# Both MLP products of a retention and MLP kernel as pairs of 64-column halves of the TensorE array

## The chip, the cores and the metric

The kernel runs on one core of a Trainium2 chip. The metric is device time in microseconds (us), median over several executions. Executions of one kernel in one job spread over 1 to 2%; a run that lies over 1.5% above the fastest of its kernel is called slow and is left out of the ratios. A comparison is given as a ratio: the mean time of one kernel's fast runs over that of the other's fast runs of the same rounds, so not quite the ratio of the medians that stand beside it.

## The reference, cut to what matters

```python
def _attn_ref(q, k, v):                       # 8 batches, 8 heads, 576 positions, 64 per head
    scores = scale * np.matmul(q, k.transpose(0, 1, 3, 2))
    ret = scores * Dmat                       # gamma_h ** (i - j) where i >= j, else 0
    return np.matmul(ret, v)

def _moe_ref(x, w_in, w_out):                 # 4608 tokens, 512 -> 2048 -> 512
    h = x @ w_in
    g = h * np.clip(h + 3.0, 0.0, 6.0) / 6.0
    return g @ w_out
```

The retention's output, heads side by side, is the MLP's input.

## The kernel before

The retention is done in chunks of 128 positions with a running state; the MLP follows in blocks of 512 tokens. Chunks and MLP are interleaved by hand: one long list of tokens fixes the order of instructions on every engine. *Tiling* means that TensorE's array (128\*128 in the profile, active rows by active columns) is used as two halves at once: row tiling (64\*128) splits the rows, column tiling (128\*64) the columns. In the kernel before, the two halves of an output pair (column tiling) or of a score pair (row tiling) mostly start 3 to 4 ns apart, and an output pair of 128 columns starts every 55.7 ns. A *semaphore* is, in the built programs, a counter that one instruction raises and another waits for. Per chunk:

- three loads on SP's DMA queue (q, k, v), and casts to 16 bit on GpSimd and VectorE;
- one transposing DMA for q and k, issued from ScalarE's queue, in ScalarE's stream (28 in all, ACTq in the profile);
- scores (row tiling, 64*128 in the profile), then outputs and state (column tiling, 128*64) on TensorE.

The MLP's two products use the whole array (128*128). ScalarE and VectorE turn each sum of the first product into g. In 8 of the 9 blocks the second product is made as seven products of sub-blocks with 256 columns (accA to accD in the profile), in the other as a plain one (po).

```python
def xpose(c):                                     # ScalarE's queue
    qk = qk16s[c]
    qt = work.tile([P, 8, P], FP16, tag="qkT", bufs=4, name="qkT")
    nc.scalar.dma_start_transpose(qt, qk.rearrange("p a h d -> p (a h d)"))
...
# outputs of the retention: two halves of 64 columns, z = 0 and 1
nc.tensor.matmul(xp[rows[z], p, :], vt[:, 2 * p + z, :], at[:, z, p, :], ...)
...
def up(kb, fc):                                   # first product of the MLP
    ph = psum.tile([P, BLK], FP32, tag="mm", bufs=4, name="ph")
    for m in range(NCC):
        nc.tensor.matmul(ph, win16[:, m, P * fc:P * fc + P], xt[:, m, :],
                         start=(m == 0), stop=(m == NCC - 1))
    hswish(ph, g[:, fc, :])                       # ScalarE, then VectorE
```

## Time and profile before

| | before |
|---|---|
| time, median of the first 3 runs | 307.52 us (304.84 to 307.79) |
| span of the profiled run | 302.4 us |
| TensorE busy | 290.4 us, 96% |
| transfers | 54 MB; the 16 DMA engines are busy nearly throughout to about 205 us |

The thing to read is that TensorE is the bound by its own busy time, and that transfers are full beside it over the first two thirds. Three of the ten lines on TensorE's waits, from the profile of before: who waited for whom, us in total, times, longest.

```profile
PE sc L283 <- ACT qkT L268: 1.1, 1, 1.1
PE xp L308 <- ACT xt L338: 1.0, 2, 0.8
PE ph L377 <- DVE g L365: 1.0, 2, 0.5
```

None of the ten is over 1.4 us in total, and all but 0.2 us lie before 77 us.

### The profile page before, as it was taken

What the parts mean: (1) busy time and instruction counts of PE and PEld (TensorE: products, weight loads), DVE (VectorE), ACT (ScalarE), POOL (GpSimd) and SP (SyncE); (2) the same over time, 40 slices, a digit from 0 to 9 for tenths busy, and PEclk for the clock granted to TensorE, in tenths of its full rate; (3) what the DMA queues carried; (4) which work ended last, traced back from release to release, by engine and by line L of the source; (5) the groups of instructions that cost most, each with busy time, mean ns of one, the idle gap of its engine ahead of it and who ended that gap; (6) DMA issues with size and microseconds to landing.
All of it is one profiled execution on the core that took longest, in us unless ns stands there. A gap on an engine that the chain in (4) does not pass through costs nothing.

```text
span 302.4 us, 7130 instructions
## 1 busy us (share of the span) xinstructions
PE 290.4 (96%) x2879; PEld 198.8 (66%) x2879; DVE 240.1 (79%) x341; ACT 145.8 (48%) x267; POOL 103.3 (34%) x116
## 2 busy tenths in 40 slices
PE   8789898998999999999999999999999999999995
PEld 3565354787788888547854786468656864684584
DVE  6765843989978999798788997998699768857963
ACT  2786705764237733565157424753467226405610
POOL 5254535776158625463843142334200000000000
PEclk9999999999999999999999999999999999999999
DMA  6999899999999999999999999997503130013003
GB/s 232 308 350 386 195 300 211 221 212 215 281 174 197 224 232 227 190 193 240 242 192 264 238 217 182 255 200 96 160 14 58 37 106 0 1 46 95 2 0 139
DMA packets 149729, 53.93 MB, mean 178 GB/s; under 512 B 134849, under 2 KB 145089, under 8 KB 149697
## 3 DMA queue, kind: packets, MB, share of 16 engines
q1 hardware_dynamic: 120128, 46.15, 69.4%
q10 hardware_dynamic: 29568, 7.34, 18.3%
q8 instruction: 22, 0.36, 0.5%
q14 instruction: 11, 0.08, 0.1%
HBM read 36.70 MB, written 9.44 MB: 153 GB/s over the span
## 4 chain that ended last, share of the span: by engine, by line
PE 85%; SPq 6%; DMA 4%; DVE 3%; ACT 1%; issue 0%
PE ph L377 29%; PE accB L491 10%; PE accA L491 9%; PE accC L491 9%; PE ph L393 8%; PE accD L491 5%; PE po L420 5%; SPq L547 4%; DMA g<-in_moe_w_out_dram 4%; PE xp L308 4%; PE sc L283 3%; PE xp L314 2%; DVE g L365 1%; DVE ss L455 1%; PE state L333 1%; SPq L248 1%
## 5 line engine op out<-in xcount | busy, mean ns | idle before, releaser
L360 ACT ACTIVATE u<-ph 128x512 f32<-128x512 f32 x144 | 84.7, 597 | 63.9 <-PE ph L377 43.8
L365 DVE SCALAR_TENSOR_TENSOR g<-u,ph 128x512 f16<-128x512 f32 x144 | 94.9, 684 | 23.8 <-ACT u L360 23.0
L377 PE MATMUL ph<-xt,win 128*128 128x512 f16 x368 | 82.5, 379 | 1.0 <-DVE g L365 1.0
L377 PEld LDWEIGHTS <-win 128*128 128x128 f16 x432 | 41.5, 98 | 49.0 <-issue 1.6
L491 PEld LDWEIGHTS <-ss 128*128 128x128 f16 x512 | 49.0, 98 | 7.1 <-DVE ss L455 1.1
L176 POOL TENSOR_TENSOR qk<-st,tq 128x512 f16<-128x512 f32 x29 | 31.7, 1095 | 49.7 <-PE state L333 17.8
L176 POOL TENSOR_TENSOR v<-st,tkv 128x512 f16<-128x512 f32 x29 | 31.7, 1097 | 36.0 <-DMA st<-in_v_dram 18.3
L294 DVE TENSOR_TENSOR at<-sc,mask 128x1024 f16<-128x1024 f32 (+1 forms) x34 | 39.0, 1154 | 4.6 <-PE sc L283 4.5
L491 PEld LDWEIGHTS <-g 128*128 128x128 f16 x384 | 36.9, 98 | 6.1 <-issue 0.8
L393 PE MATMUL ph<-xt,win 128*128 128x256 f16 x288 | 33.1, 273 | 0.0
L176 POOL TENSOR_TENSOR qk<-st,tkv 128x512 f16<-128x512 f32 x26 | 28.7, 1105 | 8.5 <-DMA st<-in_k_dram 8.2
L491 PE MATMUL accA<-wout,g 128*128 128x256 f16 x256 | 30.6, 273 | 0.8 <-DVE g L365 0.8
L491 PE MATMUL accB<-tmat,ss 128*128 128x256 f16 x256 | 30.7, 273 | 0.2 <-DVE ss L455 0.2
L393 PEld LDWEIGHTS <-win 128*128 128x128 f16 x288 | 27.6, 98 | 3.6
L338 ACT ACTIVATE xt<-xp 128x512 f16<-128x512 f32 x32 | 19.1, 597 | 19.2 <-PE xp L314 16.6
L455 DVE TENSOR_TENSOR ss<-g 128x1024 f16<-128x1024 f16 (+1 forms) x30 | 23.6, 799 | 0.3
L308 PE MATMUL xp<-at,v 128*64 128x128 f16 x288 | 20.2, 225 | 1.2 <-ACT xt L338 1.0
L308 PEld LDWEIGHTS <-v 128*64 128x64 f16 x288 | 14.4, 109 | 6.9 <-issue 3.5
L511 ACT COPY osb<-accA 128x512 f32<-128x512 f32 x8 | 4.7, 586 | 28.4 <-PE accA L491 28.4
L344 ACT CAST s<-state 64x256 f16<-64x256 f32 x48 | 17.3, 361 | 0.5
L420 PE MATMUL po<-wout,g 128*128 128x512 f16 x64 | 15.0, 379 | 0.6 <-DVE g L365 0.5
L491 PE MATMUL accC<-tmat,ss 128*128 128x256 f16 x128 | 15.4, 273 | 0.0
(88 smaller groups left out, 270.4 us busy)
## 6 DMA issues: line engine op xcount, KB each, us to landing
st<-in_v_dram SPq DMA_DIRECT2D x32, 256.0 KB, 6.4
out_dram<-osb SPq DMA_DIRECT2D x32, 256.0 KB, 4.5
st<-in_q_dram SPq DMA_DIRECT2D x28, 256.0 KB, 5.6
st<-in_k_dram SPq DMA_DIRECT2D x28, 256.0 KB, 5.7
wst<-in_moe_w_in_dram SPq DMA_DIRECT2D x4, 512.0 KB, 7.3
tmat<-in_moe_w_in_dram SPq DMA_DIRECT2D x4, 512.0 KB, 8.0
wst<-in_moe_w_out_dram SPq DMA_DIRECT2D x4, 512.0 KB, 12.5
g<-in_moe_w_out_dram SPq DMA_DIRECT2D x4, 512.0 KB, 6.5
```

Of the source, the lines that this page charges most:

```text
L176: eng.tensor_tensor(out=dst, in0=st[:, ix, :, :], in1=tab.unsqueeze(2).to_broadcast([P, H, D]), op=ALU.mult)
L294: nc.vector.tensor_tensor(out=dst, in0=src, op=ALU.mult, in1=m[:, :].unsqueeze(1).to_broadcast([P, n, P]))
L308: nc.tensor.matmul(xp[rows[z], p, :], vt[:, 2 * p + z, :], at[:, z, p, :], start=(p == 0), stop=False, skip_group_check=True)
L338: nc.scalar.activation(xts[b][:, :, t * P:(t + 1) * P], xp, ACTF.Copy, scale=0.125)
L344: nc.scalar.copy(s16[rows[z], :, rows[z]], sp[rows[z], :, :])
L360: nc.scalar.activation(u, ph, ACTF.Relu, bias=0.5, scale=1.0 / 6.0)
L365: nc.vector.scalar_tensor_tensor(out=dst, in0=uv, scalar=1.0, in1=pv, op0=ALU.min, op1=ALU.mult)
L377: nc.tensor.matmul(ph, win16[:, m, P * fc:P * fc + P], xt[:, m, :], start=(m == 0), stop=(m == NCC - 1))
L393: nc.tensor.matmul(ph[:, 256 * j:256 * j + 256], win16[:, m, P * fc:P * fc + P], xt[:, m, cs], start=(m == 0 and j == 0), stop=(m == NCC - 1),
L420: nc.tensor.matmul(po, g[:, fc, P * mc:P * mc + P], wout16[:, fc, :], start=(fc == 0), stop=(fc == NFC - 1))
L455: nc.vector.tensor_tensor(out=dst, in0=a, in1=c, op=op)
L491: nc.tensor.matmul(ps[:, m, :], lhs(fc, m), rhs[:, fc, :], start=(first and fc == 0 and m == 0), stop=(fc == HF - 1 and m == 1), skip_grou ...
```

## The change

Its intent: where MLP matmuls meet the retention's outputs and states, TensorE changes its tiling, at 94 ns from the full array to columns and 103 ns back in the kernel before. With the MLP in the same 128*64 tiling those changes fall away. Four call sites change alike; one is shown.

```diff
+    def mul(ps, lhs, rhs, start, stop):
+        for z in range(2):
+            nc.tensor.matmul(ps[z * D:z * D + D], lhs[:, z * D:z * D + D], rhs,
+                             start=start, stop=stop, skip_group_check=True)
+
     def up(kb, fc, nwarm=0):
 ...
         for m in range(NCC):
-            nc.tensor.matmul(ph, win16[:, m, P * fc:P * fc + P], xt[:, m, :],
-                             start=(m == 0), stop=(m == NCC - 1))
+            mul(ph, win16[:, m, P * fc:P * fc + P], xt[:, m, :],
+                m == 0, m == NCC - 1)
 ... (the same in up_half, the plain down product and the seven products)
```

More of the change, by code (lines that the diff above doesn't have):

```diff
@@ L392, in up_half @@
             for m in range(NCC):
-                nc.tensor.matmul(ph[:, 256 * j:256 * j + 256],
-                                 win16[:, m, P * fc:P * fc + P], xt[:, m, cs],
-                                 start=(m == 0 and j == 0), stop=(m == NCC - 1),
-                                 skip_group_check=True)
+                mul(ph[:, 256 * j:256 * j + 256],
+                    win16[:, m, P * fc:P * fc + P], xt[:, m, cs],
+                    m == 0 and j == 0, m == NCC - 1)
         d = fcs[1] - fcs[0]
@@ L419, in down_plain_part @@
             for mc, po in enumerate(pos):
-                nc.tensor.matmul(po, g[:, fc, P * mc:P * mc + P],
-                                 wout16[:, fc, :],
-                                 start=(fc == 0), stop=(fc == NFC - 1))
+                mul(po, g[:, fc, P * mc:P * mc + P], wout16[:, fc, :],
+                    fc == 0, fc == NFC - 1)
     def down_plain_end(kb, pos):
@@ L490, in product @@
             for m in range(2):
-                nc.tensor.matmul(ps[:, m, :], lhs(fc, m), rhs[:, fc, :],
-                                 start=(first and fc == 0 and m == 0),
-                                 stop=(fc == HF - 1 and m == 1),
-                                 skip_group_check=True)
+                mul(ps[:, m, :], lhs(fc, m), rhs[:, fc, :],
+                    first and fc == 0 and m == 0, fc == HF - 1 and m == 1)
         if name == "P1":
```

## The prediction

> **What bounds the kernel now.** I read the page's engine shares first, then its slices, then the chain of work that ended last, then busy time by stretch, and last the timeline of TensorE around its changes of tiling.
>
> ```profile
> PE 290.4 (96%) x2879; PEld 198.8 (66%) x2879; DVE 240.1 (79%) x341; ACT 145.8 (48%) x267; POOL 103.3 (34%) x116
> PE   8789898998999999999999999999999999999995
> DVE  6765843989978999798788997998699768857963
> PEclk9999999999999999999999999999999999999999
> PE 85%; SPq 6%; DMA 4%; DVE 3%; ACT 1%; issue 0%
> ```
>
> TensorE is busy for 96% of the span at its full granted clock, and 85% of the chain that ended last is its matmuls. The other 15% is queue, transfer and some VectorE work, all of the first 31 us but for a few pieces up to 77 us (at 68.8 us the chain goes through ScalarE and VectorE for 8.6 us while the first sums for the second product are built). Stretches, each with busy time of TensorE, weight loads, VectorE, ScalarE and GpSimd, then clock and transfers:
>
> ```profile
> 31.00:77.00 46.00, 42.92 (x405) 28.71 (x403) 35.39 (x49) 24.29 (x41) 27.61 (x26) 1.00 1.13 224
> 77.00:122.00 45.00, 44.79 (x594) 37.80 (x593) 40.39 (x50) 20.08 (x40) 23.37 (x22) 1.00 1.31 222
> 122.00:183.00 61.00, 61.00 (x619) 40.22 (x618) 52.67 (x71) 30.07 (x57) 27.17 (x25) 1.00 1.24 221
> 183.00:245.00 62.00, 62.00 (x647) 41.19 (x645) 53.17 (x75) 30.34 (x58) 11.54 (x12) 1.00 0.63 119
> 245.00:302.00 57.00, 53.61 (x365) 35.26 (x362) 38.93 (x55) 21.60 (x37) 0.00 (x0) 1.00 0.17 50
> ```
>
> From 77 to 298 us TensorE is hardly ever idle as the profile counts it (61.00 us busy of 61.00, 62.00 of 62.00). But ends of matmuls are modelled: a 128x256 matmul is listed with 273 ns while the next one starts 109 ns later, so lost time hides under "busy". Only start times show it:
>
> ```profile
> 98.82 0.49 PE L393 MATMUL ph<-xt,win 128*128 128x256 f16 x3
> 99.24 0.41 PE L308 MATMUL xp<-at,v 128*64 128x128 f16 x8
> 99.49 0.29 PE L333 MATMUL state<-v,qk 128*64 128x64 f16 x8
> 99.71 0.40 PE L283 MATMUL sc<-qkT 64*128 64x128 f16 x8
> 100.04 5.41 PE L393 MATMUL ph<-xt,win 128*128 128x256 f16 x48
> 105.38 0.25 PE L308 MATMUL xp<-at,v 128*64 128x128 f16 x2
> 105.46 0.22 PE L314 MATMUL xp<-qkT,s 128*64 128x128 f16 x2
> ```
>
> Columns: start, length, line, and before the shape the tiling. The 48 matmuls of the MLP (128*128) last 5.41 us with one modelled tail of 0.273, so one starts every (5.41 - 0.273)/47 = 0.109 us. The last starts at 105.18; the output matmul (128*64) follows at 105.38, 0.20 later instead of 0.109: 0.09 us are lost at the change of tiling. I did the same for every pair of successive starts in the trace, taking off N/2.4 + 2.4 ns for a stream of N columns. Inside a tiling the median rest is 0 ns (a pair of 64-column halves counted as one). At a change it is, by kind: full array to columns 94 ns (14 times), columns to full 103 (26), full to rows 96 (25), rows to full 96 (13), rows to columns 93 (22), columns to rows 103 (10). That is 110 changes; at these medians 10.7 us, some 3.5% of the span, with the few long waits for data that fall on a change left out.
>
> [...] 93 to 104 ns per change, and output pairs 128 columns long start every 55.7 ns, what one full matmul of that length would take (128/2.4 + 2.4). [...] The trace has 110 ns for a load of 64 columns against 98 for a full one of 128; yet the state pairs (64 columns long) start every 32 ns with two such loads per pair, so loads overlap and don't bind at 109 ns. [...] the trace has 109.1 ns for 256 and 215.8 for 512. [...]
>
> **The change part by part.**
>
> 1. *Doubled instructions, same streaming.* 1680 full MLP matmuls (432 of the up product and 64 of the plain down product with 512 columns; 288 up halves and 896 of the seven-product down part with 256) become 3360. Each pair streams the same columns through both halves of the array at once. If the second starts within 2 to 4 ns of the first, as the output pairs do, a pair takes the 109.1 or 215.8 ns of the full matmul: change 0.
>
> 2. *Changes of tiling removed.* The order of the program stays; VectorE, ScalarE, GpSimd and the queues keep their instructions. Where MLP and outputs or states meet, both are now 128*64: all 26 columns-to-full and 13 of the 14 full-to-columns changes go (the 14th follows a transpose). 3 of these lie before 31 us, where loads set the pace. On the path: 24 x 103 + 12 x 94 = 2.47 + 1.13 = 3.60 us.
>
> 3. *Changes that stay under another name.* The scores remain 64*128. 22 full-to-rows become columns-to-rows (96 to 103 ns: +0.15 us), 12 rows-to-full become rows-to-columns (96 to 93: -0.04).
>
> 4. *Changes added.* Transposes on TensorE and warm-up matmuls stay 128*128, and now sit alone between MLP matmuls: 5 columns-to-full and 3 net full-to-columns, 8 in all, counted in the instruction order of the new kernel. Two, around the warm-up at 22.6 us, are in the load-bound part. 6 x 98 = +0.59 us.
>
> 5. *First pair after a change.* The second output pair after a change starts 80 ns after the first, not 56 (+24), and after a change to the full array the second matmul comes 10 ns late. Entries to columns go from 36 to 38 and those to the full array from 39 to 6, so at most 33 x 10 ns = 0.3 us are won; I count 0.1.
>
> Sum: -3.60 + 0.15 - 0.04 + 0.59 - 0.1 = -3.0 us. Changes fall from 110 to 79, 31 x 98 ns = 3.04, the same by another count. All of it falls between 31 and 245 us; after that only MLP remains and nothing changes.
>
> Does it reach the end? TensorE waits for next to nothing from 77 us on, and must not run into its suppliers when it is ahead by up to 3 us. The transposed q and k of each chunk land 2.5 to 11.5 us before their scores start (smallest 2.52 at 123.9 us, 2.90 at 208.6, 2.82 at 231.1); at 124 us it is ahead by only about 1.2 us, at 231 by almost 3 (but loads and buffers freed by TensorE move forward too). VectorE is at most 90% busy in any stretch (40.39 of 45 us). I take nearly all as kept: about 302.4 - 3.0 = 299.4 us of profiled span.
>
> **The rivals.**
> *The feed of instructions.* A 256-column pair asks for four instructions in 109 ns, 54.5 ns per matmul. [...] The densest stretch before is 256 instructions from 111.86 us in 6.67 us, 26 ns each with no stall; [...] I give it 5%.
> *Pairs a little dearer.* 1680 pairs times 2 ns of extra start-up is 3.4 us and would eat the whole gain: about 307.5. Against it: the output pairs show 55.7 ns, no extra.
> *Pairs a little cheaper.* If each half ran on without the fixed 2.4 ns, 1680 x 2.4 = 4.0 us more would be won: about 300. The same 55.7 ns speaks against it.
> *Gain lost in waits.* If VectorE, 90% busy from 77 to 122 us, takes up part of it, 1 to 2 us remain: about 306.
>
> **Range and chances.** The three times before are 307.52, 304.84 and 307.79, and the profiled run took 304.54: two levels 3 us apart, as large as the effect. From the median, 307.52 - 3.0 = 304.5; since the new runs may fall on either level, I say 304.3, with 301 to 309 as the range. Faster by over 2% needs 6.2 us, twice the sum: 0.04. Slower by over 2% needs the feed to bind or pairs to cost 5 ns more: 0.09. Within 2%: 0.87.
>
> **What would show it right or wrong.** Right: 79 changes of tiling of 93 to 104 ns each, none between MLP and outputs or states; 256-column pairs of the MLP still start every 109 ns and 512-column ones every 216; the last stretch, from the first matmul of the up product after the last output to the end, keeps its length; the span is shorter by about 3 us, gathered evenly from 31 to 245 us. Wrong: [...] second halves that start well after the first (no overlap); pauses between MLP matmuls at steady distances (fetching of a doubled program); weight loads that stretch far beyond 110 ns; or new TensorE waits for VectorE or the transposed q and k.

The N/2.4 + 2.4 ns in it is an estimate, the line through starts in the trace of the kernel before: 109.1 ns for 256 columns and 215.8 for 512. At 128 columns it gives 55.7 ns, and 62 of the 74 spacings between full-array matmuls of that length (TensorE's transposes) are 55 or 56 ns there.

## The result, and the profile after

| | before | after |
|---|---|---|
| median, 4 runs each | 306.18 us | 315.69 us (314.07 to 316.40) |
| ratio after / before | | 1.030 (95%: 1.022 to 1.039) |
| span of the profiled run | 302.4 us | 313.5 us |

The change makes the kernel 3% slower. The page of the changed kernel: busy time, TensorE by slices, its granted clock, and the chain that ended last.

```profile
PE 292.2 (93%) x4559; PEld 222.5 (71%) x4559; DVE 238.1 (76%) x341; ACT 143.3 (46%) x267; POOL 103.7 (33%) x116
PE   8799998998999979829899999999999999999994
PEclk9979999999999999968999999999999999999999
PE 73%; DMA 6%; DVE 5%; SPq 5%; ACT 4%; POOL 3%; issue 2%; ACTq 1%; POOLq 0%
```

TensorE has a hole of which there was none before: slices 15 to 20 of 40, 110 to 157 us, with a "2" at its worst. The granted clock drops just after it, to 0.6 as the mean of slice 18. The chain has lost 12 points of TensorE, and the time from 94 to 139 us now runs through SP's queue, loads, casts and a transpose. So the first look says it is not the matmuls. Who makes TensorE wait now:

```profile
PE ph L361 <- DVE g L371: 6.7, 2, 6.3
PE sc L283 <- DMA qkT<-qk: 2.1, 1, 2.1
PE accB L361 <- DVE ss L459: 2.0, 3, 0.9
```

One wait of 6.3 us and several of 1 to 2 us. The matmuls themselves do what was predicted. Timeline of TensorE, columns as in the prediction:

```profile
103.74 1.26 PE L361 MATMUL ph<-xt,win 128*64 128x256 f16 x20
104.83 0.22 PE L308 MATMUL xp<-at,v 128*64 128x128 f16 x2
...
105.28 0.29 PE L333 MATMUL state<-v,qk 128*64 128x64 f16 x8
105.40 1.92 PE L361 MATMUL accA<-wout,g 128*64 128x256 f16 x32
107.25 0.40 PE L283 MATMUL sc<-qkT 64*128 64x128 f16 x8
```

The MLP follows the four state pairs (32 ns each from 105.28, so 0.13 us) at 105.40: no change of tiling is paid there. I sorted all start times from 60 us on, as in the prediction, with a pair counted as one, and split the time between starts:

| from 60 us to the last matmul, us | streaming | changes of tiling | waits | half clock | rest | sum |
|---|---|---|---|---|---|---|
| before | 226.5 | 8.6 (89) | 1.3 | 0.0 | 2.0 | 238.4 |
| after | 226.8 | 5.4 (56) | 13.1 | 1.8 | 2.1 | 249.1 |

Streaming is the same, the changes of tiling give 3.2 us back as forecast, and waits take 11.8 us and the clock 1.8. The clock drop comes after the idleness: the trace's clock records have half the clock (0.50) from 136.3 to 143.1 us, beginning 3.8 us after the last matmul before the 6.3 us, and the ten 512-column pairs that follow mostly start 427 ns apart instead of 216. The kernel before has no such wait and no such drop between 60 us and its end. That the one causes the other is read from this order, not tested.

**Where the longest wait comes from.** TensorE waits for VectorE, and VectorE for ScalarE:

```profile
138.39 1.88 DVE L371 SCALAR_TENSOR_TENSOR g<-u,ph 128x512 f16<-128x512 f32 x3 [6.93 <-ACT u L366]
```

ScalarE around that time, before and then after; ACTq is its queue, which issues the transpose in order with the activations:

```profile
125.90 1.29 ACT L360 ACTIVATE u<-ph 128x512 f32<-128x512 f32 x2
126.67 1.25 ACTq L184 DMA_TRANSPOSE qkT<-qk  x1
128.03 1.75 ACT L360 ACTIVATE u<-ph 128x512 f32<-128x512 f32 x3 [0.83 <-DVE g L365]
```

```profile
129.46 1.08 ACT L366 ACTIVATE u<-ph 128x512 f32<-128x512 f32 x2
135.81 1.85 ACTq L184 DMA_TRANSPOSE qkT<-qk  x1
137.76 2.06 ACT L366 ACTIVATE u<-ph 128x512 f32<-128x512 f32 x4 [7.22 <-issue]
```

Before, the 13th transpose goes out 0.1 us after the last activation has started. After, it stands in ScalarE's stream from 130 to 135.8 us, and the activations behind it stand with it: 7.22 us of idleness, which the profile can only call "issue". Its casts were ready: the last one of that chunk began at 119.25 and took 2.02 us. So it waited for something that is neither a cast nor an engine.

The built programs tell what. Each has 208 DMAs, 180 on SP's queue and 28 on ScalarE's, and each DMA raises one of eight semaphores at its landing, 26 DMAs to a semaphore. In the common order of both queues the eight come in turn, all 208 times in both programs. From the ninth on, a DMA first waits until the DMA that had its semaphore before has landed: this wait is written out for all 200 in the changed kernel and for 199 of 200 in the kernel before. The streams of ScalarE, VectorE, GpSimd and SP are the same in both programs, instruction by instruction. But the common order is not: the transposes stand elsewhere among SP's 180 DMAs. The number, counted from 0, of SP's DMA that stands just ahead of each of the 28 transposes:

```
transpose   1  2  3  4  5  6  7  8  9 10 11 12  13  14  15  16  17 ...  21  22 ... 28
before     42 44 50 51 58 60 66 72 76 77 81 86  91  96 103 107 114     136 141    155
after      44 46 53 56 62 64 71 80 83 85 89 93 101 106 112 117 124     146 150    155
later by    2  2  3  5  4  4  5  8  7  8  8  7  10  10   9  10  10      10   9      0
```

In these programs a later place means that the semaphore was held by a later DMA. The 13th transpose now waits for the landing of this SP issue (the first of the two):

```profile
129.82 1.84 SPq L161 DMA_DIRECT2D st<-in_k_dram  x2
```

By the trace's record it landed at 135.74 us; the transpose went out at 135.81. In the kernel before, the holder ahead of it had landed 3.07 us before ScalarE came to it. Of the 28 transposes, 9 go out within 0.12 us of such a landing in the changed kernel (of five loads, three stores and one transpose), and none in the kernel before (the two nearest come 0.16 and 0.22 us after it).

**Why the build reorders.** Only the TensorE instructions differ, so something that the build derives from them sets the order; its own estimate of TensorE's time is the likeliest. Built without running: pairs in the first product alone move the 13th transpose by 5, in the second alone by 4, in both by 10. An estimate that counts the two halves one after the other would fit this, but this is argued.

### The profile page after: what moved, and what is told of

Its sections match the earlier page's. It is cut to its first block, busy times and chain, and to the rows that moved or that the text cites.

```text
span 313.5 us, 10492 instructions
## 1 busy us (share of the span) xinstructions
PE 292.2 (93%) x4559; PEld 222.5 (71%) x4559; DVE 238.1 (76%) x341; ACT 143.3 (46%) x267; POOL 103.7 (33%) x116
## 4 chain that ended last, share of the span: by engine, by line
PE 73%; DMA 6%; DVE 5%; SPq 5%; ACT 4%; POOL 3%; issue 2%; ACTq 1%; POOLq 0%
PE ph L361 32%; PE accB L361 8%; PE accC L361 7%; PE accA L361 7%; PE po L361 4%; PE accD L361 4%; SPq L156 4%; DVE g L371 3%; PE xp L308 2%; DMA st<-in_v_dram 2%; PE sc L283 2%; DMA st<-in_k_dram 2%; PE xp L253 2%; DVE ss L459 2%; DMA st<-in_q_dram 2%; POOL qk L176 2%
## 5 line engine op out<-in xcount | busy, mean ns | idle before, releaser
L361 PE MATMUL ph<-xt,win 128*64 128x512 f16 (+1 forms) x1312 | 118.2, 337 | 6.8 <-DVE g L371 6.7
L361 PEld LDWEIGHTS <-win 128*64 128x64 f16 x1440 | 82.0, 111 | 48.4 <-issue 9.5
L361 PEld LDWEIGHTS <-ss 128*64 128x64 f16 x1024 | 54.8, 110 | 4.5 <-DVE ss L459 4.3
L361 PEld LDWEIGHTS <-g 128*64 128x64 f16 x896 | 48.6, 110 | 7.6 <-issue 1.2
L176 POOL TENSOR_TENSOR qk<-st,tkv 128x512 f16<-128x512 f32 x26 | 29.4, 1129 | 10.1 <-DMA st<-in_k_dram 5.9
L361 PE MATMUL accB<-tmat,ss 128*64 128x256 f16 x512 | 30.8, 273 | 2.0 <-DVE ss L459 2.0
L361 PE MATMUL accA<-wout,g 128*64 128x256 f16 x512 | 30.7, 273 | 0.0
L361 PE MATMUL accC<-tmat,ss 128*64 128x256 f16 x256 | 15.7, 273 | 0.6 <-DVE ss L459 0.6
L283 PE MATMUL sc<-qkT 64*128 64x128 f16 x256 | 12.7, 219 | 3.2 <-DMA qkT<-qk 2.1
L361 PE MATMUL po<-wout,g 128*64 128x512 f16 x128 | 15.1, 380 | 0.6 <-DVE g L371 0.5
L361 PE MATMUL accD<-tmat,g 128*64 128x256 f16 x256 | 15.4, 273 | 0.0
```

The lines of the kernel that those rows point to most:

```text
L176: eng.tensor_tensor(out=dst, in0=st[:, ix, :, :], in1=tab.unsqueeze(2).to_broadcast([P, H, D]), op=ALU.mult)
L283: nc.tensor.matmul(sc[z][:, p, :], qt[z * D:z * D + D, HP + p, :], qt[z * D:z * D + D, p, :], start=True, stop=True)
L361: nc.tensor.matmul(ps[z * D:z * D + D], lhs[:, z * D:z * D + D], rhs, start=start, stop=stop, skip_group_check=True)
```

## The experiments

Theory 1: the loss is in the places of the transposes in the common order of DMAs, through the shared semaphores. Theory 2: the loss is in the pairs, either their number or their feed or the lead that they give TensorE over its suppliers.

To separate them, the places are pinned by ordering edges that exist in the build alone and add no wait on the chip. The other 4 engines keep the hand-made order, SP's DMAs are chained in their traced order. With the old places the full-array kernel builds to the same streams and waits as the kernel before, which shows that the pinning by itself changes nothing.

```diff
+    PLACE = [42, 44, 50, ...]
+    for y, x in zip(sp_list, sp_list[1:]):
+        tc.add_manual_dep(x.ins, y.ins.name, nosync, reason="as traced")
+    for x, n in zip(xp_dma, PLACE):
+        tc.add_manual_dep(x.ins, sp_list[n].ins.name, nosync, reason="place")
+        if n + 1 < len(sp_list):
+            tc.add_manual_dep(sp_list[n + 1].ins, x.ins.name, nosync, reason="place")
```

All runs below have right results unless said otherwise.

### Each kernel with the other's places

The changed kernel with the places of before:

> The changed kernel, all MLP matmuls as pairs, but the 28 transposing DMAs of ScalarE stand in the build's common order of DMAs where the kernel before had them, so the eight completion semaphores are dealt out as before. Theory 1 (the loss is in the places: each DMA waits for the landing of the one that had its semaphore before, and in the changed kernel the transposes stand up to 10 DMAs later and so wait for later loads, with ScalarE stuck behind them): about 303 us, 3 less than the kernel before, and no TensorE wait over 2 us after 60 us. Theory 2 (the loss is in the pairs themselves: instructions twice as many, their fetching, or TensorE running ahead of its suppliers): still 313 to 317 us.

The kernel before with the places of the changed kernel:

> The kernel before, full-array MLP matmuls, but the transposing DMAs stand where the changed kernel has them. Theory 1: slow like the changed kernel or a little slower, 313 to 319 us, with a wait of TensorE of several us near 130 to 140 us that goes back to a transpose on ScalarE's queue. Theory 2: as before, 305 to 308 us.

| MLP | places | median us | ratio to before |
|---|---|---|---|
| pairs | old | 304.0 | 0.995 (0.990 to 0.999) |
| full array | new | 314.19 | 1.030 (1.025 to 1.034) |

The times go with the places and not with the matmuls. The full array at the new places is as slow as the changed kernel, with a 5.2 us wait of TensorE at 137 us. Theory 2 falls as the cause of the 3%. It keeps a share: by the same split by start times, one profile each, the full array at the new places has 8.6 us of waits and 1.3 us at half clock, the pairs at the same places 13.1 and 1.8, which the 3.2 us of fewer changes of tiling only partly pay for. Some waits come with the pairs. One execution of the pairs, the profiled one, took 1031.54 us, with the matmuls several times slower (the 512 of accA from wout and g were busy for 110.0 us, 30.7 in the changed kernel) and no clock line on its page; it is a disturbed execution that I can't explain, and it is set aside. The other five were 303.07 to 304.85.

### Half of the shift, and other doses

> The changed kernel with each transposing DMA half way between its old and its new place (0 to 5 DMAs later than before instead of 0 to 10). Theory 1: between the two, 303 to 310 us, with shorter waits at fewer places. Theory 2: still 313 to 317 us.

310.08 us, ratio 1.015 (1.009 to 1.021): half the shift, half the loss.

Three earlier than before, and two later:

> The pairs with every transposing DMA up to the 21st standing 3 DMAs earlier than in the kernel before. If only late places hurt, 302 to 304 us, as good as the old places or better. If the old places are a balance (an early place makes a later load wait for the transpose instead), slower than the old places: 304 to 308 us, with longer waits of SP for transposes.

> The pairs with the transposing DMAs standing 2 DMAs later than in the kernel before. Half way (0 to 5 later) gave 310 and the old places 304, so by the dose 304 to 308 us; 302 to 304 if the old places are on the early side of the best.

Three earlier: 310.37 us, 1.013 (1.006 to 1.020), above the 304 to 308 that I had expected for a balance. SP's queue then waited 28.7 us in sum for transposes, against 6.6 us at the old places (profile of the repeated run below), 13.4 in the kernel before and none in the changed kernel: the old places are a balance, and an early transpose holds up the load that gets its semaphore next. Two later: 308.13 us, ratio 1.000 (0.990 to 1.010); unclear, as its runs spread from 305 to 310, and the slowest of the four counts as slow and isn't in the ratio. How many transposes are held does not measure the loss: here nine went out within 0.12 us of the landing that they waited for, as many as in the changed kernel. How long ScalarE stands does better: its longest idle time just before a held transpose is 2.2 us here, 5.3 in the changed kernel and 8.5 in the next run.

### One transpose alone

> The kernel before (full array) with one transposing DMA, the 13th, placed 10 DMAs later, as the changed kernel has it (the 14th moves 5 to stay behind it). Theory 1: the 13th is issued near 135 us instead of 126.7, when the load that had its semaphore before has landed; ScalarE stands still from about 127 to 135, TensorE runs out of free accumulators and waits 4 to 8 us, and the whole is 308 to 313 us. Theory 2: 304 to 307 us, no such wait.

```diff
-    PLACE = [..., 81, 86,  91,  96, 103, ...]
+    PLACE = [..., 81, 86, 101, 101, 103, ...]
```

317.31 us, ratio 1.036 (1.029 to 1.043): one misplaced transpose (and the one behind it) costs as much as all of the changed kernel's (1.030; the intervals overlap). My 308 to 313 was too low. ScalarE, then TensorE's longest wait, in this run:

```profile
126.06 1.29 ACT L369 ACTIVATE u<-ph 128x512 f32<-128x512 f32 x2
135.89 2.91 ACTq L193 DMA_TRANSPOSE qkT<-qk  x1
138.90 2.06 ACT L369 ACTIVATE u<-ph 128x512 f32<-128x512 f32 x4 [11.55 <-DMA out_dram<-osb]
```

```profile
PE ph L386 <- DVE g L374: 10.9, 2, 10.1
```

The transpose went out at 135.89, 0.07 us after the landing at 135.82 of the load that held its semaphore. ScalarE stood still for 11.55 us, TensorE for 10.1, and 2.5 us more went to the half clock. The line names a store as what ended ScalarE's wait; that store, out_dram, was not what the transpose waited for by the built program. So the name that the profile gave for the end of this wait was not its cause.

### Where the rest of the 3 us went

With the old places the pairs win 0.3 to 0.5% in three jobs, 1.0 to 1.6 us, not the 3.0 predicted. Two more runs of the same kernel, the first for a profile in an undisturbed execution:

> The pairs with the transposing DMAs at their old places once more, because the profile of its first run fell into a disturbed execution of 1029 us. Expected: 303 to 305 us again, and a profile that tells where the rest of the predicted 3 us went: if the 79 changes of tiling cost 93 to 104 ns each and a 256-column pair takes 109 ns, the missing 1.5 us must show as waits of TensorE or as time at a lower clock; if the pairs are dearer, as a pair period above 109.1 or 215.8 ns.

> The pairs at the old places a third time, for the size of their gain with all loads: 303 to 305.5 us, a ratio of 0.993 to 0.998 to the kernel before.

305.30 us, 0.997 (0.990 to 1.004), and 304.75 us, 0.996 (0.992 to 1.000). The split by start times of the first: streaming 226.9, changes of tiling 5.4, waits 5.7 us where the kernel before has 1.3. The largest of them:

```profile
PE sc L292 <- DVE at L303: 2.3, 2, 2.0
```

The longest ends at 119.00 us, when VectorE has masked the scores of the chunk before and so freed their place. That mask stood behind a cast of q in VectorE's order. The cast in the kernel before, and here:

```profile
113.78 1.04 DVE L176 TENSOR_TENSOR qk<-st,tq 128x512 f16<-128x512 f32 x1
```

```profile
117.12 0.69 DVE L185 TENSOR_TENSOR qk<-st,tq 128x512 f16<-128x512 f32 x1 [3.59 <-issue]
```

It waited for its load of q: issued at 109.82 and landed at 117.04 us, in the kernel before at 107.41 and 112.10. The transpose for the scores that waited was late too: it went out at 107.72 us, 0.40 us earlier than in the kernel before, but landed at 116.67 and not 113.97. So transfers were to be taken out of the way, in both kernels alike. Their outputs are wrong, which doesn't matter for the times. From the 10th chunk on v is not loaded and its cast reads k. The places are counted again over the DMAs that are left, so the semaphores have other holders too.

```diff
+            if ix == 2 and no_v(c):          # from the 10th chunk on
+                sp_list.extend([None] * (1 + c[0]))
+                continue
... (cut)
-        eng.tensor_tensor(out=dst, in0=st[:, ix, :, :],
+        src = 1 if ix == 2 and c in order and no_v(c) else ix
+        eng.tensor_tensor(out=dst, in0=st[:, src, :, :],
```

> Wrong results on purpose: the kernel before (full array, old places) without the loads of v from the 10th chunk on (the cast of v reads k's stage instead), so that transfers have slack. All engines keep their instructions. If transfers cost the kernel before little, 300 to 304 us. It is the base for the next run.

> The same without the loads of v, but with the MLP as pairs, at the same places. If the 3 us of saved changes of tiling were eaten by late transfers in the run with all loads (where 1 to 1.6 us were kept), here all of it is kept: 2.5 to 3.2 us less than the full array without v, and no TensorE wait over 0.5 us after 80 us. If the pairs lose the rest by themselves, again only 1 to 1.6 us less.

| without loads of v, old places | median us | ratio to before |
|---|---|---|
| full array | 304.36 | 0.995 (0.991 to 0.999) |
| pairs | 301.38 | 0.986 (0.982 to 0.989) |

The pairs now win 304.36 - 301.38 = 2.98 us, the predicted sum. After 80 us TensorE has no wait over 0.5 us; in the split its waits are 1.2 us in all. In neither of these two profiles does a transpose go out within 0.12 us of the landing that it waits for. So the run shows that the rest was lost to DMAs, but not how much of it to slow transfers and how much to held semaphores. A long run of pairs in this profile also bears on the feed of instructions:

```profile
98.61 0.40 PE L299 MATMUL sc<-qkT 64*128 64x128 f16 x8
98.93 5.43 PE L377 MATMUL ph<-xt,win 128*64 128x256 f16 x96
104.20 0.22 PE L324 MATMUL xp<-at,v 128*64 128x128 f16 x2
```

48 pairs: (5.43 - 0.273)/47 = 0.110 us each from first to last, as the 48 full matmuls of before, and the output follows without the 0.09 us lost before. The feed does not bind in this run of 96 matmuls. What one instruction costs was not measured.

### A version to beat both

> A version meant to beat both kernels: the pairs at the old places, but the five transposing DMAs that in the profile of the pairs at old places were still issued within 0.1 us of the landing that they waited for (the 11th, 12th, 20th, 21st and 24th) stand one DMA earlier. If those waits are what holds the pairs back, 302 to 304 us, a ratio of 0.988 to 0.994; if the transfers are simply full and another wait takes their place, 303 to 306 us as at the old places.

> The same idea spread: the 10th to the 24th transposing DMA all one earlier (the 23rd not). 302 to 305 us if one earlier is on the good side; 305 to 308 us if already one earlier makes the loads wait for transposes, as three earlier did (310).

304.39 us, 0.995 (0.990 to 1.000), and 304.25 us, 0.997 (0.991 to 1.004). No better than the old places, as far as these intervals tell: in the profile of the first, two transposes are still held, one of them another than before. No correct version is clearly better than the pairs at the old places, which are about 0.4% under the kernel before (ratios 0.995, 0.997 and 0.996 in three jobs).

## Why the prediction was wrong, point by point

- *Same streaming.* Right. 256-column pairs start every 109.5 ns against 109.4 for full matmuls, 512-column pairs every 216.1 ns in both, with weight loads of 64 columns listed at 110 to 111 ns in the mean; the second half starts 3 ns after the first in the median. (In some 140 of the 1680 pairs it starts 20 ns or more after it, one of the prediction's signs of being wrong, but the periods stay the same, so nothing is lost.) The stretch after the last output, 368 matmuls or pairs, takes 53.91 us against 53.88.
- *Changes of tiling removed, kept, added.* Right: all 79 changes of the program are in the trace, at 93 to 103 ns by kind; 3.2 us less from 60 us on, and with transfers out of the way 3.0 us less in the end.
- *"The order of the program stays; VectorE, ScalarE, GpSimd and the queues keep their instructions."* **This is the step that failed.** It is true of the instructions and was taken to be true of their waits. The build gave the DMAs other semaphores, 9 transposes then went out only when an earlier DMA had landed, and ScalarE's stream stood behind them. The changed kernel has 11.8 us more of TensorE waits and 1.8 us of half clock; the full array at the same places alone has 7.3 and 1.3. The comparison of the two programs listed differences on VectorE, ScalarE, GpSimd and SP, and I put them down to shifted line numbers (my own account). The prediction's last sign of being wrong, "new TensorE waits for VectorE or the transposed q and k", is what came: 6.7 and 2.1 us.
- *"Does it reach the end?"* Also wrong, in size, even with the old places. I measured how early a transpose lands before its scores (2.5 us or more) and took that as the margin. The margin that shrinks first is the one between the landing that a transpose waits for and ScalarE's arrival there. With the pairs at the old places 5 transposes went out within 0.12 us of that landing (8 in the profile of the third job), none before. A third to a half of the 3.0 us was kept.
- *The rivals.* A feed that binds and dearer or cheaper pairs are refuted by the periods above. "Gain lost in waits" was the right kind, but I named VectorE and stopped at 306 us. A longer wait than the one removed was in no rival.
- *The range*, 301 to 309, left out the one rival beyond it (the feed, 5%; how far beyond was not shown by any trace). All rivals looked at TensorE or at VectorE behind it; none asked what else the build makes anew. That slower by over 2% had a chance of 0.09 is no credit: it was given for the feed and for dearer pairs.

## What to carry to other kernels

Where a build orders the DMAs and hands out their semaphores itself, as here, a change to one engine can change the waits of the others (here the transposes stood up to 10 DMAs later, and 9 of them went out only at the landing that they waited for): compare the built programs' waits, not only their instructions, before predicting that "nothing else moves". A transpose issued from ScalarE's queue held up ScalarE's work behind it while it waited for a semaphore (ScalarE stood for 7.22 us in the changed kernel and 11.55 us with one transpose late), so ask of each such DMA what it waits for and how early that is done. When a change looks bad, run the old code with the new side effects and the new code with the old ones before judging its idea.
